# A fused retention and Mish feed-forward kernel on one core: four buffers for scaled v, w_in's third piece in two, one first-layer block in another PSUM bank, six products no longer in halves

## The chip, the core and the metric

The kernel runs on one core of a Trainium2 chip. A core has a matrix engine (TensorE, "PE" in the profile; its weight loads have a row of their own, "PEld"), three engines for elementwise work (VectorE "DVE", ScalarE "ACT", GpSimd "POOL") and a queue engine (SyncE, "SP") that mostly issues transfers. TensorE writes to PSUM, eight banks of 128 partitions x 512 float32; the other operands live in SBUF. The engines run beside each other and wait for each other by semaphores; transfers between the device's memory and SBUF run on 16 DMA engines that all queues share. The metric is the device time of one execution in microseconds (us), the median of several.

## The reference, cut to what matters

```python
# q, k, v: (8, 8, 576, 64) float32: batch, head, position, head dimension
scores = np.matmul(q, k.transpose(0, 1, 3, 2)) / np.sqrt(64)
gamma  = 1.0 - 2.0 ** (-5.0 - np.arange(8))
Dmat   = np.where(rel >= 0, gamma[:, None, None] ** rel, 0.0)   # rel = i - j
attn   = np.matmul(scores * Dmat, v)
x = attn.transpose(0, 2, 1, 3).reshape(4608, 512)
h = x @ w_in                               # (512, 2048)
g = h * np.tanh(np.log1p(np.exp(h)))       # Mish
out = g @ w_out                            # (2048, 512)
```

There is no softmax: a score is only multiplied by a power of gamma that falls with the distance. So a row can be computed from its own block of positions and a running sum ("state") of k times v over the earlier ones, with gamma's power split into a factor for q and its inverse for v. That v, times its inverse factor, is "scaled v", `vs` in the kernel.

## The kernel before, in words

**Tiling.** The 4608 token rows are 36 chunks of 128 rows, nine tiles of four chunks. The first eight chunks (tiles 0 and 1) are the first 128 positions of each of the eight batches, and have code of their own (`f_...`); the other 28 go through `step_p` (scale q and cast q and k to `qks`, on DVE), `step_v` (scale v to `vs`, line 301: on DVE for chunks below 20, on POOL from 20 on), `step_t` (transposes, on TensorE for chunks below 18, by transfers from SP after that), and, two chunks at a time, `visit`. A visit makes on TensorE the new states of chunks n+2 and n+3 (`states`, line 392), the outputs of chunks n and n+1 from scores and scaled v (`outputs`, line 451), their rest from the states (`outputs_end`, line 468) and the next scores (`step_s`, line 337): several hundred small matmuls within some 1.4 us. The outputs go to two PSUM banks and are cast from there to `xT`, one half on ACT and one on DVE (`outputs_copy`, line 480).

**The feed-forward layers.** `g1(t, f)` makes one 128 x 512 block of the first layer for tile t: four accumulating products over the 512 input features into a PSUM bank `hp`, then Mish on ACT (line 541) into `gT`. There are 16 blocks to a tile. `g2` makes the second layer for 128 rows from 16 products. After the visit, `g1` needs the two `hp` banks that the visit's outputs held.

**Products in halves.** `product` issues one matmul with 512 columns, or, while a counter `halved[0]` is above zero and the product is neither the first nor the last of its sum, two matmuls with 256 columns each, each with a weight load of its own (lines 520 to 523). Work and result are the same; the program has one load and one matmul more.

**The PSUM pools** are `ps_sc` (tiles of two banks, two of them), `ps_st` (one bank), `ps_h` (two banks, `hp`) and `ps_o` (one bank, `ops`).

**The order of the work** is written out by hand: the calls stand in the order in which each engine gets them, and a tile pool makes an instruction wait where it would overwrite a buffer that is still read. The POOL queue holds the casting transfers (w_in, w_out and the first q and k, float32 in memory and bf16 in SBUF), all the other loads of q, k and v, some elementwise work and, from chunk 20 on, `step_v`. Its transfers share eight semaphores in turn, so that each waits until the one eight places before it has landed. w_in arrives in pieces along its 2048 columns: 256, 256, 512 (the third), 512 and 512; block f of `g1` needs columns 128f to 128f + 127.

**Where the change is.** Pool `tok` (line 66) holds `vs`, five buffers. At the start (lines 665 to 669) the 16 blocks of tile 0 run:

```python
    for f in range(2):
        g1(0, f, 2, begun[f])
    for f in range(2, nF):
        halved[0] = 2 if f > 3 else 1
        g1(0, f)
```

In the loop over the tiles from 2 on, `n` is the chunk whose visit is next and `w` the place within its eight steps. At `w` of 0 and 1 `step_v` is called for chunks n+2 and n+3, a little after the visit of n-2; the visit of n comes at `w` of 6; at `w` of 5 DVE scales one v for a state (`f_state`, line 254, result `v0s`), for n from 16 to 22 only.

Of the kernel before, what the change touches and what calls it, by code (L numbers as in the profile page):

```python
# [9 lines left out]
F32 = mybir.dt.float32  # L10
# [6 lines left out]
def kernel(  # L17
# [21 lines left out]
    P = 128  # L39
# [5 lines left out]
    NCH = 4  # L45
# [17 lines left out]
    wpool = ctx.enter_context(tc.tile_pool(name="weights", bufs=1))  # L63
    first = ctx.enter_context(tc.tile_pool(name="first", bufs=1))
    io = ctx.enter_context(tc.tile_pool(name="io", bufs=PF))
    tok = ctx.enter_context(tc.tile_pool(name="tok", bufs=5))
    tr = ctx.enter_context(tc.tile_pool(name="tr", bufs=4))
    xp = ctx.enter_context(tc.tile_pool(name="xp", bufs=2))
    gp = ctx.enter_context(tc.tile_pool(name="gp", bufs=2))
# [4 lines left out]
    ps_h = ctx.enter_context(tc.tile_pool(name="ps_h", bufs=2, space=PS))  # L74
    ps_o = ctx.enter_context(tc.tile_pool(name="ps_o", bufs=1, space=PS))
# [9 lines left out]
    def load_w_in(f0, n):  # L85
        nc.gpsimd.dma_start(out=w_in_t[:, :, ds(f0, n)], in_=w_in_r[:, :, ds(f0, n)])
# [22 lines left out]
    def load_first_v(b):  # L109

        if b < 4:
            pair = stage[:, ds(8 + 2 * b, 4), :].bitcast(F32).rearrange("p a (c d) -> p (a c) d", d=D)
        else:
            pair = first.tile([P, 2 * H, D], F32, name="vpair", bufs=2)
        for e in range(2):
            v0[b + e] = pair[:, ds(H * e, H), :]
        nc.gpsimd.dma_start(out=pair, in_=v[ds(b, 2), :, 0:P, :].rearrange("b h p d -> p (b h) d"))
# [23 lines left out]
            load_first_qk(0, i, b)  # L141
    load_first_v(0)
    load_first_v(2)
    for f0, n in ((0, 256), (256, 256), (512, 512)):
        load_w_in(f0, n)
    mask = consts.tile([P, 64], F32)
    lg = [math.log(1.0 - 2.0 ** (-5.0 - h)) for h in range(H)]
# [108 lines left out]
    def load_k0(b):  # L256
        k0r[b] = first.tile([P, H, D], F32, name="k0r", bufs=2)
        nc.gpsimd.dma_start(out=k0r[b], in_=k[b, :, 0:P, :].rearrange("h p d -> p h d"))

    def cast_k0(b, copy=nc.scalar.copy):  # L260
        k0[b] = first.tile([P, H, D], BF16, name="k0", bufs=3)
        copy(k0[b], k0r[b])
# [3 lines left out]
    def load(n, gate=None):  # L266
        if n >= n_chunks:
            return
        b, c = chunks[n]
        qkr = io.tile([P, 2, H, D], F32, name="qkraw")  # L270
        vr = io.tile([P, H, D], F32, name="vraw", bufs=7)
        live[n] = {"qkr": qkr, "v": vr}
        for t, src in ((qkr[:, 0], q), (qkr[:, 1], k), (vr, v)):
            if c < 4:
                ins = nc.gpsimd.dma_start(  # L275
                    out=t, in_=src[b, :, ds(P * c, P), :].rearrange("h p d -> p h d"))
                if gate is not None:
                    behind(ins, gate)
                    gate = None
            else:  # L280
                for e in range(2):
                    nc.gpsimd.dma_start(
                        out=t[ds(64 * e, 64)],
                        in_=src[b + e, :, ds(512, 64), :].rearrange("h p d -> p h d"))
# [151 lines left out]
    def run(jobs, *how):  # L436
        while jobs:
            jobs.pop()(*how)
# [45 lines left out]
    def hold(n):  # L484

        nc.gpsimd.tensor_copy(held[:, n % 2:n % 2 + 1], live[n]["qk"][:, 1, NP - 1, P - 1:P])  # L486

    def visit(n, banks, copies, between=None):


        units, early = states(n + 2)
        if units:
            units[0]()
        both = outputs(n, banks)
        seen = written(outputs_end(n, both, 0))
        if units:
            step_s(n + 2)
        elif between:
            between()
        for unit in units[1:early]:  # L500
            unit()
        outputs_end(n, both, 1, seen)
        for unit in units[max(early, 1):]:
            unit()
        outputs_copy(n, both, copies)
        if units:
            step_m(n + 2)

    outs = {}
    halved = [0]  # L510
# [4 lines left out]
    def product(to, w, x, first, last):  # L515
        if first or last or not halved[0]:
            newest[0] = nc.tensor.matmul(to, lhsT=w, rhs=x, start=first, stop=last)  # L517
            return
        halved[0] -= 1
        n = x.shape[-1] // 2  # L520
        for j in range(2):
            nc.tensor.matmul(to[:, ts(j, n)], lhsT=w, rhs=x[:, ts(j, n)], start=False, stop=False,  # L522
                             skip_group_check=True)

    def g1_half(f):
        hp = ps_h.tile([P, NCH * P], F32, name="hp")
        n = NCH * P // 2
        for c in range(KC):
            nc.tensor.matmul(hp[:, 0:n], lhsT=w_in_t[:, c, ts(f, P)], rhs=xts[0][:, c, 0:n],
                             start=(c == 0), stop=(c == KC - 1))  # L530
        return hp

    def g1(t, f, parts=1, begun=None):
        if t not in gts:
            gts[t] = gp.tile([P, nF, NCH * P], BF16, name="gT")
        hp = ps_h.tile([P, NCH * P], F32, name="hp") if begun is None else begun
        n = NCH * P // parts
        for j in range(0 if begun is None else 1, parts):
            for c in range(KC):
                product(hp[:, ts(j, n)], w_in_t[:, c, ts(f, P)], xts[t][:, c, ts(j, n)], c == 0, c == KC - 1)  # L540
        done = nc.scalar.activation(gts[t][:, f, :], hp, AX.Mish)  # L541
        if (t, f) in gated:
            load(gated[t, f], done)
            queued[0] += 1
# [18 lines left out]
    def stores(copy=nc.vector.tensor_copy):  # L563
        while ready:
            store(*ready.pop(), copy)
# [35 lines left out]
    def att(n, steps):  # L601
        if n >= n_chunks:
            return
        for step in steps:
            {"P": step_p, "V": step_v, "T": step_t}[step](n)
# [33 lines left out]
    begun = [g1_half(0), g1_half(1)]  # L639
# [25 lines left out]
    for f in range(2):  # L665
        g1(0, f, 2, begun[f])
    for f in range(2, nF):
        halved[0] = 2 if f > 3 else 1
        g1(0, f)
    for i in range(2):  # L670
        f_mix(0, i)
# [1 line left out]
    for i in range(nF):  # L673
        for step in steps.get(i, "").split():
            n = int(step[1])
# [77 lines left out]
    for t in range(2, nT + 1):  # L753
        for i in range(nF):
            n, w = NCH * (t + 1) + i // 8 * 2, i % 8
            if w == 2 and n in cast_at:
                cast_k0(cast_at[n])
            if w == 2:
                run(casts, act)
                halved[0] = {20: 32}.get(n, 0)  # L760
            if w == 6 and n + 4 == NPE:
                load_k0(3)
                att(n + 4, "T")
                att(n + 5, "T")
            if w == 6 and n < n_chunks:
                visit(n, ((ps_h, "hp"), (ps_h, "hp")), (act, dve), lambda: g2(t - 1, i))
            if w == 0:
                stores(act if n == N0 + 4 else dve)
                run(sums)
            if w == 7 and n + 2 == NPE:  # L770
                stores()
            if w in (0, 1) and n + 2 < NPE:
                att(n + 2 + w, "P")
            if w in (4, 5) and n + 4 >= NPE:
                stores()
                att(n + w, "P")
            if w in ((3, 4) if n + 2 < NPE else (0, 1)):
                att(n + 2 + (w in (1, 4)), "V")
            if w == 5 and 16 <= n < 24:
                f_state(1, n // 2 - 8, nc.vector)  # L780


            if w == 7 and n + 4 == NPE:
                hold(n + 4)
                hold(n + 5)
                more_loads(n + 7)
            if w == 1 and NPE < n + 2 < n_chunks:
                hold(n + 2)
            if w == 1 and n + 2 >= NPE:
                more_loads(n + 7)  # L790
                if t in (3, 4):
                    load_k0(2 * t - 2 + i // 8)
            if w in (4, 5) and n + 2 < NPE:
                att(n - 2 + w, "T")
            stores()


            if t == 2:
                if w == 6:
                    g2(1, 8 + i // 2)  # L800
                g1(t, i)
                if i % 2 and w != 7:
                    g2(1, 8 + i // 2)
            elif t == nT:
                if i < 12:
                    g2(t - 1, i)
            elif w == 6:

                last = n < n_chunks <= n + 2
                g2(t - 1, i + last)  # L810
                g1(t, i)
                if NPE < n + 4 < n_chunks:
                    for x in (4, 5):
                        step_t(n + x, newest[0])
            elif w == 7 and n < n_chunks <= n + 2:
                g1(t, i)
            elif i % 4 == 0:
                g1(t, i)
                g1(t, i + 1)
                g2(t - 1, i)  # L820
            else:
                if i % 4 != 1:
                    g1(t, i)
                g2(t - 1, i)
# [32 lines left out]
```

## Time and profile before

| | |
|---|---|
| median of three runs | 300.78 us (300.23 to 300.98) |
| the profiled execution | 302.5 us, of which its span (first to last instruction) 300.8 |
| TensorE busy | 288.6 us, 96% of the span |
| VectorE, ScalarE, GpSimd busy | 147.6, 134.9, 133.3 us |
| granted TensorE clock | 1.000 over the span |
| moved by DMA | 47.45 MB, 160 GB/s over the span |
| instruction queue (q8) | 27 transfers, 0.44 MB |

A line of a time view has the start and the duration in us, engine, line of the kernel, operation, output <- inputs, shape and the number of instructions merged into it; in brackets stands how long the engine was idle before it and what ended that. "issue" means that nothing in the profile explains the wait. A matmul's end is modelled, so neighbouring matmuls overlap in the view; the distance between their starts (0.216 us for 512 columns in a dense stretch, since four follow in 0.86 us) is the better measure.

### The profile page before, as it was taken

How to read it: one execution, taken by the hardware profiler on the slowest of the kernel's cores; microseconds unless marked ns; L12 is line 12 of the kernel's file. 1: busy time of each engine (PE TensorE's matmuls, PEld its weight loads, DVE VectorE, ACT ScalarE, POOL GpSimd, SP SyncE). 2: the span in 40 equal slices, each digit the busy share in tenths (PEclk: the TensorE clock that was granted, in tenths of full speed). 3: DMA queues.
4: the chain of work that ended last, by engine and by line, in shares of the span. 5: the costliest groups of instructions: out<-in, count | busy, mean ns of one | idle time of the engine just before them, and what ended most of it. 6: DMA issues, size and time to landing. Idle time of an engine off the chain costs nothing.

```text
span 300.8 us, 7911 instructions
## 1 busy us (share of the span) xinstructions
PE 288.6 (96%) x3450; PEld 157.1 (52%) x3488; DVE 147.6 (49%) x237; ACT 134.9 (45%) x221; POOL 133.3 (44%) x173
## 2 busy tenths in 40 slices
PE   7889999999899999999999999999999999999995
PEld 3456787555455545456744454545454544444443
DVE  5722547597939548472849363727363312011011
ACT  5557325876557552534353435343535342433200
POOL 8675856767464294836575724656110000000000
PEclk9999999999999999999999999999999999999999
DMA  7999999999998679878977858876714110110131
GB/s 152 210 206 206 203 238 222 340 227 198 250 218 218 141 205 206 212 188 151 213 192 199 202 129 144 210 179 173 107 37 105 37 37 35 37 35 35 51 91 71
DMA packets 39619, 47.45 MB, mean 158 GB/s; under 512 B 21792, under 2 KB 28448, under 8 KB 39584
## 3 DMA queue, kind: packets, MB, share of 16 engines
q0 software_dynamic: 14896, 32.25, 48.7%
q1 hardware_dynamic: 24544, 14.49, 20.5%
q8 instruction: 27, 0.44, 0.7%
q10 hardware_dynamic: 144, 0.20, 0.2%
q14 instruction: 8, 0.07, 0.1%
HBM read 38.80 MB, written 9.44 MB: 160 GB/s over the span
## 4 chain that ended last, share of the span: by engine, by line
PE 84%; DVE 5%; DMA 4%; issue 3%; POOL 3%; DVEq 0%; POOLq 0%
PE hp L517 38%; PE ops L517 29%; PE hp L522 5%; DMA w_in_t<-in_moe_w_in_dram 4%; DVE qks L294 3%; PE ops L522 2%; PE sc L315 1%; PE hp L585 1%; PE sc L337 1%; POOL gT L106 1%; PE st L522 1%; PE sc L392 1%; PE hp L468 1%; DVE v0s L254 1%; PE hp L451 1%
## 5 line engine op out<-in xcount | busy, mean ns | idle before, releaser
L517 PE MATMUL hp<-xT,w_in_t 128*128 128x512 bf16 (+1 forms) x512 | 128.2, 376 | 3.1 <-DVE xT L480 1.0
L541 ACT ACTIVATE gT<-hp 128x512 bf16<-128x512 f32 x144 | 86.0, 598 | 94.2 <-PE hp L517 87.7
L517 PE MATMUL ops<-w_out_t,gT 128*128 128x512 bf16 x417 | 103.2, 379 | 1.9 <-issue 1.9
L517 PEld LDWEIGHTS <-w_in_t 128*128 128x128 bf16 x532 | 51.7, 98 | 57.0 <-issue 2.3
L517 PEld LDWEIGHTS <-gT 128*128 128x128 bf16 x484 | 46.1, 98 | 52.7
L593 DVE COPY res<-ops 128x512 f32<-128x512 f32 x28 | 19.3, 690 | 88.4 <-PE ops L517 88.4
L294 DVE TENSOR_TENSOR qks<-qkraw,gqk 128x512 bf16<-128x512 f32 x56 | 42.6, 815 | 4.1 <-DMA qkraw<-in_k_dram 4.1
L275 POOL DMA_DIRECT2D qkraw<-in_q_dram x24 | 21.5, 894 | 13.4 <-ACT gT L541 8.4
L486 POOL COPY held<-qkT 128x1 bf16<-128x1 bf16 x10 | 1.9, 187 | 51.6 <-DMA qkT<-qks 51.6
L301 POOL TENSOR_TENSOR vs<-vraw,gv 128x512 bf16<-128x512 f32 x16 | 18.3, 1148 | 10.7 <-PE hp L451 10.5
L275 POOL DMA_DIRECT2D vraw<-in_v_dram x24 | 21.2, 884 | 3.1 <-DMA vpair<-in_v_dram 1.5
L275 POOL DMA_DIRECT2D qkraw<-in_k_dram x24 | 21.2, 884 | 2.5 <-DMA w_out_t<-in_moe_w_out_dram 1.3
L480 ACT CAST xT<-hp 128x512 bf16<-128x512 f32 x14 | 8.2, 586 | 28.1 <-PE hp L468 26.9
L480 DVE CAST xT<-hp 128x512 bf16<-128x512 f32 x13 | 8.9, 688 | 21.9 <-PE hp L468 16.7
L428 DVE TENSOR_TENSOR total<-sc,total 128x256 f32<-128x256 f32 x40 | 16.9, 422 | 1.0
L343 DVE TENSOR_TENSOR sm<-sc,mask 128x1024 bf16<-128x1024 f32 x14 | 17.0, 1214 | 0.6 <-PE sc L337 0.6
L522 PEld LDWEIGHTS <-gT 128*128 128x128 bf16 x152 | 14.5, 98 | 3.0
L522 PE MATMUL hp<-xT,w_in_t 128*128 128x256 bf16 x96 | 14.6, 272 | 0.0
L522 PEld LDWEIGHTS <-w_in_t 128*128 128x128 bf16 x96 | 9.4, 98 | 6.1 <-issue 0.6
L431 ACT CAST ssb<-total 128x768 bf16<-128x768 f32 (+3 forms) x13 | 11.7, 897 | 1.7 <-DVE total L428 1.6
L517 PE MATMUL hp<-w_out_t,gT 128*128 128x512 bf16 x49 | 12.0, 379 | 0.2 <-issue 0.2
L392 PE MATMUL sc<-vs,qks 64*64 64x64 bf16 x384 | 9.7, 197 | 0.0
(120 smaller groups left out, 259.1 us busy)
## 6 DMA issues: line engine op xcount, KB each, us to landing
out_dram<-res SPq DMA_DIRECT2D x31, 256.0 KB, 3.8
qkraw<-in_q_dram POOLq DMA_DIRECT2D x24, 256.0 KB, 5.0
qkraw<-in_k_dram POOLq DMA_DIRECT2D x24, 256.0 KB, 5.4
vraw<-in_v_dram POOLq DMA_DIRECT2D x24, 256.0 KB, 5.7
w_out_t<-in_moe_w_out_dram POOLq DMA_DIRECT2D x4, 512.0 KB, 11.2
k0r<-in_k_dram POOLq DMA_DIRECT2D x8, 256.0 KB, 7.1
w_in_t<-in_moe_w_in_dram POOLq DMA_DIRECT2D x3, 512.0 KB, 11.1
gT<-in_k_dram POOLq DMA_DIRECT2D x8, 128.0 KB, 6.8
```

Source lines behind the costliest of these rows:

```text
L275: ins = nc.gpsimd.dma_start(out=t, in_=src[b, :, ds(P * c, P), :].rearrange("h p d -> p h d"))
L294: nc.vector.tensor_tensor(slots[:, :, y], heads[:, :, y], factors[:, :, y].unsqueeze(3).to_broadcast([P, NP, 2, D]), op=OP.mult)
L301: engine.tensor_tensor(vs, live[n]["v"], gv[:, c, :].unsqueeze(2).to_broadcast([P, H, D]), op=OP.mult)
L343: nc.vector.tensor_tensor(sm.rearrange("p e x n i -> p (e x n) i"), live[n]["sc"].rearrange("p e x n i -> p (e x n) i"), mask.unsqueeze(1) ...
L392: ins = nc.tensor.matmul(to, lhsT=ks, rhs=vs, start=(x is not None or j == 0 and p == 0), stop=True, skip_group_check=True)
L428: nc.vector.tensor_tensor(new[:, k], st[:, j, x], total[b], op=OP.add)
L431: casts.append(lambda copy: copy(lows[:, 0:k], new[:, 0:k]))
L480: copy(xts[t][:, :, ds(P * s, 2 * P)].rearrange("p h (x j i) -> p j h x i", x=2, j=2)[:, j], both[j])
L517: newest[0] = nc.tensor.matmul(to, lhsT=w, rhs=x, start=first, stop=last)
L522: nc.tensor.matmul(to[:, ts(j, n)], lhsT=w, rhs=x[:, ts(j, n)], start=False, stop=False, skip_group_check=True)
L541: done = nc.scalar.activation(gts[t][:, f, :], hp, AX.Mish)
L593: copy(ot, ops)
```

## The change

Four edits. Scaled v gets four buffers instead of five. The third piece of w_in (columns 512 to 1023) is loaded by two transfers of 256 columns. Block 2 of tile 0's first layer is accumulated in the `ops` bank instead of an `hp` bank. And six products that were issued as two halves are issued whole: one each in blocks 4, 5 and 6 of tile 0, and three of the 32 that follow in the stretch after `n == 20`.

```diff
-    tok = ctx.enter_context(tc.tile_pool(name="tok", bufs=5))
+    tok = ctx.enter_context(tc.tile_pool(name="tok", bufs=4))
...
-    for f0, n in ((0, 256), (256, 256), (512, 512)):
+    for f0, n in ((0, 256), (256, 256), (512, 256), (768, 256)):
         load_w_in(f0, n)
...
-        hp = ps_h.tile([P, NCH * P], F32, name="hp") if begun is None else begun
+        if begun is not None:
+            hp = begun
+        elif (t, f) == (0, 2):
+            hp = ps_o.tile([P, NCH * P], F32, name="ops")
+        else:
+            hp = ps_h.tile([P, NCH * P], F32, name="hp")
...
     for f in range(2, nF):
-        halved[0] = 2 if f > 3 else 1
+        halved[0] = 2 if f > 6 else 1
         g1(0, f)
...
             if w == 2:
                 run(casts, act)
-                halved[0] = {20: 32}.get(n, 0)
+                halved[0] = {20: 29}.get(n, 0)
```

## The prediction

> **What bounds the kernel now.** I read the engines' totals first, then TensorE's waits, then the time view around each, then the chain of waits. TensorE is busy for 96% of the span at full clock:
>
> ```profile
> PE 288.6 (96%) x3450; PEld 157.1 (52%) x3488; DVE 147.6 (49%) x237; ACT 134.9 (45%) x221; POOL 133.3 (44%) x173
> ```
>
> So only the places where TensorE stands still can be won. Its waits after the start (engine, line, what it waited for; us, times, longest):
>
> ```profile
> PE hp L517 <- DVE xT L480: 1.0, 3, 0.4
> PE hp L517 <- issue: 0.8, 2, 0.6
> PE hp L517 <- DMA w_in_t<-in_moe_w_in_dram: 0.4, 1, 0.4
> ```
>
> From about 21 us the chain of waits runs through TensorE to the end, save three stretches through DVE that end in these three xT waits. What TensorE gains early therefore reaches the end, unless one of those stretches starts from something else. It does not: each begins with a DVE copy released by a product (110.38 us, behind "PE ops"). I size a standstill by the distance between the starts of neighbouring matmuls or weight loads, less the normal 0.216 us (0.11 behind a half).
>
> *Place 1, the third piece of w_in.* Block 4 needs it; POOL's row shows when the next piece has landed, since its transfer waits for that:
>
> ```profile
> 19.71 0.59 PE L517 MATMUL hp<-xT,w_in_t 128*128 128x512 bf16 x2
> 20.68 0.39 PE L517 MATMUL hp<-xT,w_in_t 128*128 128x512 bf16 x1 [0.38 <-DMA w_in_t<-in_moe_w_in_dram]
> 23.71 0.59 POOL L106 DMA_DIRECT2D gT<-in_k_dram  x1 [0.90 <-PE hp L517]
> ```
>
> The two products start at 19.71 and 19.92, so block 4 could start at 20.14 and starts at 20.68: 0.54 lost.
>
> *Place 2, the instruction stream.* Block 2 of tile 2 stops in the middle of one sum, with nothing to wait for; a smaller stop lies inside the visit at 68 us:
>
> ```profile
> q8 instruction: 27, 0.44, 0.7%
> 68.10 0.26 PEld L337 LDWEIGHTS <-qkT 64*64 64x64 bf16 x21 [0.20 <-issue]
> 79.85 0.59 PE L517 MATMUL hp<-xT,w_in_t 128*128 128x512 bf16 x2
> 81.04 1.46 PE L517 MATMUL hp<-xT,w_in_t 128*128 128x512 bf16 x6 [0.59 <-issue]
> ```
>
> 27 transfers for TensorE's 6,976 loads and matmuls are one per 258 instructions, so a block has about 256. Counted in the trace, the loads that come late at 68.10 and 81.04 are the 736th and the 992nd: 256 loads, so 512 instructions, two blocks apart. I read both as the first instructions of blocks that came too late. The transfer before the second ran from 78.31 to 79.62, after two dense visits (67.2 and 74.3 us) had used some 500 instructions. The distance between the loads is 0.97, so 0.75 is lost there and about 0.3 at 68.10.
>
> *Place 3, POOL's scaling against DVE's scaling.* The visit at 114 us:
>
> ```profile
> 113.85 2.22 POOL L301 TENSOR_TENSOR vs<-vraw,gv 128x512 bf16<-128x512 f32 x2
> 113.87 0.43 PE L451 MATMUL hp<-sm,vs 64*64 64x64 bf16 x32
> 114.09 2.53 DVE L254 TENSOR_TENSOR v0s<-vpair,gv 128x512 bf16<-128x512 f32 x1
> 116.54 0.68 DVE L480 CAST xT<-hp 128x512 bf16<-128x512 f32 x1
> 117.27 1.02 PE L517 MATMUL hp<-xT,w_in_t 128*128 128x512 bf16 x4 [0.27 <-DVE xT L480]
> ```
>
> The scaling v0s takes 0.68 elsewhere and 2.53 here, ending just behind POOL's two scalings: it stood until POOL was done. The cast behind it frees the hp bank late. The same happens at 147.93 and 163.82. The starts are 0.64, 0.56 (behind a half) and 0.79 apart: 0.42 + 0.45 + 0.57 = 1.44 lost. At 130 us the order is the other way and nothing is lost:
>
> ```profile
> 130.00 0.68 DVE L254 TENSOR_TENSOR v0s<-vpair,gv 128x512 bf16<-128x512 f32 x1
> 130.00 1.58 POOL L301 TENSOR_TENSOR vs<-vraw,gv 128x512 bf16<-128x512 f32 x1 [1.08 <-PE hp L451]
> 130.69 0.69 DVE L480 CAST xT<-hp 128x512 bf16<-128x512 f32 x1
> ```
>
> DVE was first, POOL took 1.58 in place of 1.06, and the cast from PSUM ran at its usual 0.69 beside POOL.
>
> **The change part by part.**
>
> *w_in's third piece in two.* Columns 512 to 767 land without waiting for the rest. From the landing of the second piece (18.34, block 2's load) to that of the third (20.64) lie 2.3 us; half is 1.15 to 1.35, so the first half lands at about 19.6, before 20.14, and the second near 20.8, before block 6 (20.14 + 1.73 = 21.87). The runs become shorter, and that costs:
>
> ```profile
> 13.00:16.00 3.00, 2.92 (x43) 1.45 (x43) 2.81 (x6) 1.65 (x4) 3.00 (x6) 1.00 1.36 193
> 16.00:20.50 4.50, 4.00 (x37) 2.58 (x32) 0.85 (x2) 2.43 (x5) 2.81 (x4) 1.00 1.26 207
> ```
>
> The last column is GB/s. From 13 to 16 us mostly the 256-column pieces move, later the wider ones: 193 against 207, 7% of some 2.3 us, 0.13 to 0.17. The fourth piece then lands at 23.66 + 0.15 and block 8, which before started at 20.68 + 4 x 0.868 = 24.15, starts at about 23.84 in place of the 23.6 that TensorE could reach. Gain 0.31. Bounds: 0.54 with no cost of the short runs; a loss of 1.5 if a piece of 256 columns always takes the 2.1 us between the first two landings (16.24 at the latest, and 18.34). I take 0.31, since the rate over 3 us is the nearer row: the first two pieces also queue behind v. On POOL one more issue (0.8) falls into its idle 2.38 before 12.77. Behind it the eight semaphores turn by one place: the last q load of the first group now waits for the second piece (18.4 in place of 16.5) and w_out's first for the new halves (about 19.6 and 20.8 in place of 18.58 and 20.92, with POOL's v0s behind each). I cost that at nothing: until 26.3, when w_in's last piece lands, the DMA engines work through a full queue, so these only join it later. Were that cover gone, the q transfer would be 1.9 late at DVE's copy of 28.36, whose result TensorE wants at 30.9; 0.5 of that is spare.
>
> *Block 2 in the ops bank.* Its first matmul started at 18.41, its weights were there at 18.34; ops has been free since 16.8. Gain 0 to 0.07; I take 0. The next user of ops is g2 at 33.97.
>
> *Six products whole.* Eight halves take 0.87 where four whole take 0.86, 0.003 for each pair: 6 x 0.003 = 0.02. What counts is the place of the blocks: three loads and three matmuls fewer stand ahead of 68 and 81 us. Each block then begins six instructions later in the work. [...] Bounds: 0.75, and a loss of 0.3 (the smaller stop once more, if another block comes late); I take 0.65, worked from the stop itself. The other three, near 140 us, move later blocks; by the trace every transfer of that queue after 83 us ends 3 us or more ahead of its block's first instruction: nothing.
>
> [...]
>
> *Four buffers for vs.* On DVE (chunks below 20) the buffer's last reader is an earlier visit, which ended 5 us or more ahead: no wait. On POOL, scaling n+2 overwrote the v of n-3, now that of n-2, so it waits for the outputs of the visit of n-2, as that of n+3 did before. The row of 130.00 shows a scaling start 0.40 behind the first such output (129.60). At the three visits that gives 114.27, 145.10 and 160.67. DVE's v0s starts at 114.09, at 144.75, and, without the lock on the qks ahead of it (4 x 0.78 behind 157.38, as at 111), at 160.4: first each time, by 0.18, 0.35 and 0.25. Then it takes 0.68, the cast follows as soon as the outputs are complete (115.1 in place of 116.54), over 1 us ahead of need. Gain 1.44. Behind the later scalings on POOL stand the copy that waits for transposes (121.22, 5.15 idle before it) and then loads: the 1 us of delay is covered by that idle time. Bounds: 1.44, and a loss of 0.9: POOL first at all three, two scalings of 1.05 from 114.27, v0s 0.55 and the cast 0.69 behind them to 117.6, against 116.85 when TensorE wants the bank: 0.8 each, 2.4 in place of 1.44.
>
> **Sum.** 0.31 + 0.02 + 0.65 + 1.44 = 2.4 off the span of 300.8: 298.4, or 300.1 with the 1.7 that lie around it in the profiled 302.5. The unprofiled median, 300.78, is the length of the span; I take off it 2.3, as the stop at 81 hangs on one transfer's queueing.
>
> **The rivals.**
> - *Partly.* One group fails: POOL is first after all (margins 0.18 to 0.35), or the stop at 81 us only moves. 300.78 - 0.96 (no gain of vs) to - 1.65 (none of the stream): 299.1 to 299.8, and 300.3 where both fail in part. For it: narrow margins, times from one execution.
> - *Nothing.* The unprofiled executions, 1.7 shorter than the profiled one, lack these stops, if the recording itself brings them about: only the 0.3 of the start, 300.5. Against it: the xT stops follow from the order on POOL and DVE, not from traffic.
> - *Slower.* The scalings of v now fall on the cast of each of the eight visits from 16 to 30. If POOL's lock stops the cast too, it ends at 0.40 + 2.1 + 0.69 = 3.2 behind the first output, where TensorE wants the bank at 2.98: 0.25 at five visits, and 0.8 at the three with a v0s, 3.65 in place of 1.44. With the other gains of 1.0 that is 302.0. It decides from the point where the cast waits 0.3 us for POOL. Against it: the cast of 130.69 took 0.69 beside POOL.
>
> **How the numbers follow.** Forecast 0.53 (297.7 to 299.4), partly 0.25 (299.1 to 300.3), nothing 0.12 (300.2 to 301.1), slower 0.10. About 0.3%, 0.9 us, is what a measurement can tell: faster is below 299.88, which takes the forecast and half of the second, 0.66; slower above 301.68, 0.10. The range runs from 297.7 to 300.9: it leaves out the slower case and some of nothing's.
>
> **What would show it.** Block 4 starts near 20.1 and block 8 near 23.8; the stop in tile 2 shrinks from 0.75 to 0.1 or so, three products later; POOL's scalings come in pairs behind the outputs of visits, v0s takes 0.68 at all four, and no xT wait of TensorE is left. It is wrong if v0s still takes 2.5, if a new "issue" stop stands elsewhere between 60 and 90 us, or if block 8 waits beyond 24.2.

## The result and the profile after

The changed kernel takes 299.61 us in the median (299.07 to 301.55) against 300.88 us for the kernel before (299.67 to 303.74): a ratio of 0.9956, with a 95% interval from 0.9938 to 0.9974. It is faster by 1.3 us, where 2.3 were forecast. The two recorded executions differ by more, 302.5 us (span 300.8) against 299.74 us (span 298.0), that is by 2.8 in both measures.

The engines' totals after:

```profile
PE 290.9 (98%) x3482; PEld 156.1 (52%) x3482; DVE 136.0 (46%) x237; ACT 134.8 (45%) x221; POOL 132.8 (45%) x174
```

DVE is busy for 11.6 us less than in the record of before, with as many instructions. Of that, 7.4 lie in the scalings of q and k (line 294) and 3.7 in v0s (line 254): they wait less inside their own time (the longest takes 0.69 and 0.68, in place of 2.52 and 2.53).

*Place 1.* The time view around blocks 3 to 5 of tile 0, and GpSimd's next k issue:

```profile
19.36 0.81 PE L517 MATMUL hp<-xT,w_in_t 128*128 128x512 bf16 x3
20.01 0.38 PE L522 MATMUL hp<-xT,w_in_t 128*128 128x256 bf16 x2
20.23 0.81 PE L517 MATMUL hp<-xT,w_in_t 128*128 128x512 bf16 x3
23.71 0.59 POOL L106 DMA_DIRECT2D gT<-in_k_dram  x1 [0.45 <-PE hp L517]
```

The third product of the first line, at 19.79, is the first of block 4: it follows without a wait, 0.9 us earlier than before (20.68). The traces also hold the updates of the transfers' semaphores, and they give the landings. Here the second piece landed at 18.00, the halves of the third at 19.30 and 20.63, the fourth at 23.17; in before the second landed at 18.30, the third at 20.64, the fourth at 23.18. So in these two records the split made neither the third piece as a whole nor the fourth later. The k issue at 23.71, the same in both, comes 0.53 behind the landing that it waits for. Block 8 starts at 23.26 (block 4 plus four times 0.868) in place of 24.15. But the lead shrinks again at 30.6, where the chain of waits (start, us, what) and TensorE's time view show a new bound:

```profile
18.56 9.80 DMA gT<-in_q_dram
28.45 2.08 DVE qbx L175
```

```profile
30.58 0.62 PE L190 MATMUL sc<-ident,qbx 128*128 128x128 bf16 x8 [0.21 <-DVE qbx L175]
```

The chain of before ran through w_in to 20.64 and from there through TensorE alone. Now it runs through a q transfer and a DVE copy, and TensorE waits for that copy: its first matmul starts 0.59 behind the product ahead of it (29.99) in place of 0.22, so 0.37 is lost. At 34 us the changed kernel is 0.52 ahead.

*Place 2.* The time view of block 2 of tile 2, where TensorE had stood for 0.75:

```profile
78.22 1.03 PE L517 MATMUL ops<-w_out_t,gT 128*128 128x512 bf16 x4
79.09 1.89 PE L517 MATMUL hp<-xT,w_in_t 128*128 128x512 bf16 x8
80.81 1.03 PE L517 MATMUL ops<-w_out_t,gT 128*128 128x512 bf16 x4
```

Eight products run through. The stop at 68 us is gone too.

*Place 3.* GpSimd's scalings, DVE's scaling v0s and its cast at the visit of 113 us, and then at that of 128 us:

```profile
111.82 0.68 DVE L254 TENSOR_TENSOR v0s<-vpair,gv 128x512 bf16<-128x512 f32 x1
112.91 2.05 POOL L301 TENSOR_TENSOR vs<-vraw,gv 128x512 bf16<-128x512 f32 x2
113.53 0.69 DVE L480 CAST xT<-hp 128x512 bf16<-128x512 f32 x1 [1.02 <-PE hp L468]
...
128.02 2.04 POOL L301 TENSOR_TENSOR vs<-vraw,gv 128x512 bf16<-128x512 f32 x2 [0.86 <-PE hp L451]
128.70 0.69 DVE L480 CAST xT<-hp 128x512 bf16<-128x512 f32 x1 [0.89 <-PE hp L468]
```

v0s takes 0.68 and begins 0.89 to 1.09 ahead of GpSimd (at all four places). GpSimd's scalings come in pairs, from 128 us on behind the outputs of the visit (line 451), and the cast runs at 0.69 in the middle of them. It waits for the outputs' last products (line 468) alone. No wait of TensorE for xT is left.

How late the record of before is against that of after, measured at the same weight load in both, gives the whole difference: 0.52 at 34 us, 0.76 at 69, 1.52 at 80, 1.99 at 117, 2.23 at 148, 2.81 at 164, and 2.78 at the end. So in these two executions the start was worth 0.52, the instruction stream 0.24 + 0.76, and the three xT stops 0.43 + 0.24 + 0.58.

### The profile page after: what moved, and what is told of

The parts are those of the page before. It is cut to its first block, busy times and chain, and to the rows that moved or that the text cites. A ratio compares the mean times of both kernels' runs of the same rounds, so it can differ in the third digit from the quotient of the medians.

```text
span 298.0 us, 7938 instructions
## 1 busy us (share of the span) xinstructions
PE 290.9 (98%) x3482; PEld 156.1 (52%) x3482; DVE 136.0 (46%) x237; ACT 134.8 (45%) x221; POOL 132.8 (45%) x174
## 4 chain that ended last, share of the span: by engine, by line
PE 89%; DMA 6%; POOL 2%; DVE 1%; issue 1%; POOLq 0%; DVEq 0%
PE hp L517 39%; PE ops L517 32%; PE hp L522 4%; DMA gT<-in_q_dram 3%; DMA w_in_t<-in_moe_w_in_dram 3%; PE ops L522 2%; PE sc L337 1%; PE sc L392 1%; PE hp L468 1%; PE sc L315 1%; PE hp L451 1%; PE hp L590 1%; POOL gT L106 1%; PE st L522 1%; POOL gT L117 1%; PE st L392 1%
## 5 line engine op out<-in xcount | busy, mean ns | idle before, releaser
L517 PE MATMUL hp<-xT,w_in_t 128*128 128x512 bf16 (+1 forms) x533 | 129.7, 376 | 0.0
L517 PE MATMUL ops<-w_out_t,gT 128*128 128x512 bf16 x432 | 106.8, 379 | 0.0
L294 DVE TENSOR_TENSOR qks<-qkraw,gqk 128x512 bf16<-128x512 f32 x56 | 35.2, 683 | 4.5 <-DMA qkraw<-in_k_dram 4.5
L301 POOL TENSOR_TENSOR vs<-vraw,gv 128x512 bf16<-128x512 f32 x16 | 16.3, 1041 | 21.3 <-PE hp L451 21.3
L522 PE MATMUL hp<-xT,w_in_t 128*128 128x256 bf16 x86 | 13.3, 273 | 0.0
L517 PE MATMUL hp<-w_out_t,gT 128*128 128x512 bf16 x52 | 12.7, 379 | 0.0
```

What stands on the lines that cost most here:

```text
L294: nc.vector.tensor_tensor(slots[:, :, y], heads[:, :, y], factors[:, :, y].unsqueeze(3).to_broadcast([P, NP, 2, D]), op=OP.mult)
L301: engine.tensor_tensor(vs, live[n]["v"], gv[:, c, :].unsqueeze(2).to_broadcast([P, H, D]), op=OP.mult)
```

## The experiments

Each kernel was compared with the kernel before on the chip on which it ran itself. The median of before on those chips was 300.43, 300.90 and 300.93, so kernels of different groups are compared by their ratios. The first group is the first four below, the second the next four, the third the last four; of these groups only the second holds the changed kernel itself. A ratio is not exactly the quotient of the two medians (0.9970 below, where 299.80 / 300.90 is 0.9963), so differences under 0.3 us can't be read from ratios. "The record" is the one execution of a kernel whose trace was kept.

### Four buffers alone

```diff
-    tok = ctx.enter_context(tc.tile_pool(name="tok", bufs=5))
+    tok = ctx.enter_context(tc.tile_pool(name="tok", bufs=4))
```

> The kernel before with four buffers for scaled v instead of five, and nothing else. Theory A (each stop is as long in every execution as in the one recorded): the three waits of TensorE for xT near 117, 148 and 164 us go, v0s takes 0.68 at all four places, and the time falls by 1.4 us, ratio 0.995. Theory B (the recorded execution of before, 302.5, was a long one of its kind, and the stops behind POOL's scalings are shorter or missing in others): the profile shows the same order of the scalings, but the median falls by 0.3 to 0.9 us only, ratio 0.997 to 0.999. Theory C (the gain of the whole change lies at the start and in the instruction stream alone): no change within 0.2%.

Median 300.01, ratio 0.9981 (0.9968 to 0.9995): theory B. The visit of this kernel at 144 us, in the time view:

```profile
143.32 0.68 DVE L254 TENSOR_TENSOR v0s<-vpair,gv 128x512 bf16<-128x512 f32 x1
144.24 2.04 POOL L301 TENSOR_TENSOR vs<-vraw,gv 128x512 bf16<-128x512 f32 x2 [1.04 <-PE hp L451]
145.05 0.69 DVE L480 CAST xT<-hp 128x512 bf16<-128x512 f32 x1 [1.05 <-PE hp L468]
```

v0s is over 0.24 before GpSimd begins, and the cast takes 0.69 beside GpSimd's scalings, clear of the lock (DVE standing until GpSimd's scalings are done, as v0s did for 2.53 in place of 0.68 at 114 us in before). No xT wait is left.

### The split of w_in alone

```diff
-    for f0, n in ((0, 256), (256, 256), (512, 512)):
+    for f0, n in ((0, 256), (256, 256), (512, 256), (768, 256)):
```

> The kernel before with the third piece of w_in loaded in two, and nothing else. Theory A: block 4 starts at about 20.1 without a wait, block 8 at 23.8, and 0.3 us is won: ratio 0.999. Theory B (the copy qbx, which waits for the q transfer at 28.4, takes most of it back): block 8 starts 0.3 to 0.6 earlier, but TensorE waits for qbx near 30.6 for most of it, and the second layer starts 0.1 to 0.5 us earlier: ratio 0.998 to 1.000. The stop in tile 2 stays (0.5 us or more), and the waits for xT stay.

Median 300.52, ratio 1.000 (0.9974 to 1.0026): too wide to tell 0.3 us. In the record block 4 runs on without a wait, as expected, but TensorE does not wait for qbx. I had expected the stop at the 992nd load to stay, and it is not there; one of 0.45 stands at the 736th. Of the three xT stops one is left, 0.34. It shows the lock with five buffers, at the visit just quoted:

```profile
141.55 0.88 POOL L258 DMA_DIRECT2D k0r<-in_k_dram  x1
142.45 2.29 POOL L301 TENSOR_TENSOR vs<-vraw,gv 128x512 bf16<-128x512 f32 x2
142.76 2.53 DVE L254 TENSOR_TENSOR v0s<-vpair,gv 128x512 bf16<-128x512 f32 x1
145.21 0.68 DVE L480 CAST xT<-hp 128x512 bf16<-128x512 f32 x1
```

Here, with five buffers, GpSimd scales as soon as its load issues are out (142.43), without a wait for a product of the visit. It was 0.31 ahead of v0s. At 112 us of the same execution it was 0.15 behind (112.34 against 112.19), v0s took 0.68, and nothing was lost.

### The six products whole, alone

```diff
-        halved[0] = 2 if f > 3 else 1
+        halved[0] = 2 if f > 6 else 1
...
-                halved[0] = {20: 32}.get(n, 0)
+                halved[0] = {20: 29}.get(n, 0)
```

> The kernel before with the six products whole, and nothing else. Theory A (the block of instructions that came too late is needed three products later, its request leaves at the same time): the stop of 0.75 in block 2 of tile 2 shrinks to about 0.1 and stands three products later, the smaller one at 68 us stays near 0.3, and the time falls by 0.65 us, ratio 0.998. Theory B (the delay of the instruction transfer changes from execution to execution by more than these three products): a stop between 0 and 0.8 is seen at the shifted place, and the median changes by less than 0.3 us. The waits for xT stay.

Median 300.63, ratio 1.0007 (0.9990 to 1.0025): theory B. The record has no stop at the 992nd load and one of 0.42 at the 736th.

### Two products more in halves

```diff
-        halved[0] = 2 if f > 3 else 1
+        halved[0] = 2 if f > 1 else 1
```

> The kernel before with two products more in halves (one in each of blocks 2 and 3 of tile 0), so that every later block of instructions begins two products earlier in the work: the other direction. Theory A: the stop in tile 2 stands two products earlier and grows by 2 x 0.216 = 0.43 to some 1.2 us; the time rises by 0.4 us, ratio 1.0015. Theory B (the delay of the transfer changes by more than that between executions): a stop between 0 and 1.2, median within 0.3 us of before's. The waits for xT stay.

Median 300.64, ratio 1.0001 (0.9980 to 1.0023). The record agrees with theory A on the place and is larger than its size:

```profile
78.88 1.03 PE L517 MATMUL ops<-w_out_t,gT 128*128 128x512 bf16 x4
81.13 1.24 PE L517 MATMUL hp<-xT,w_in_t 128*128 128x512 bf16 x5 [1.23 <-ACT ssb L431]
```

The stop stands ahead of the block's first product, two products earlier than before's, at the 992nd load again; 1.60 lies between the loads, so 1.38 is lost. (The line names ACT's copy ssb. That it was the instruction stream is argued, from the count of loads and from the transfer on its queue that ended at 79.75: the load came 1.38 behind it, and the 992nd load of before 1.42 behind its own.) There is no stop at 736, and one of 0.33 at the 864th load. The median is theory B's.

### The changed kernel once more

> The changed kernel once more, beside the kernels that leave one part of it out, on the same chip. Theory A (the forecast: 2.3 us): ratio 0.992. Theory B (the first comparison: 1.3 us, because the recorded execution of before was a long one): ratio 0.994 to 0.997. Its profile shows whether the stop in the instruction stream is gone for good (A: nothing over 0.15 at the 992nd load, 0.3 at the 736th) or varies (B: anything from 0 to 0.8 at either), and whether the waits for xT are gone again (both theories: yes).

Median 299.80, ratio 0.9970 (0.9956 to 0.9984): theory B, a gain of 1.1 us. The record has stops of 0.34 at the 736th load and of 0.33 at the 864th, none at the 992nd, and no xT wait.

### The changed kernel with five buffers

```diff
-    tok = ctx.enter_context(tc.tile_pool(name="tok", bufs=4))
+    tok = ctx.enter_context(tc.tile_pool(name="tok", bufs=5))
```

> The changed kernel with five buffers for scaled v, as before. Theory A (three xT stops of the recorded length in each execution): 1.4 us above the changed kernel. Theory B (four buffers alone were worth 0.4 to 0.7 us): 0.4 to 0.7 above the changed kernel, ratio to before 0.996 to 0.998. Theory C (the parts help only together): no gain left, ratio 1.000. In the profile v0s takes 2.5 again at three places in A, at one to three in B.

Median 300.07, ratio 0.9976 (0.9958 to 0.9993), 0.27 above the changed kernel on the same chip: below theory B's lower end, far from A. The intervals of the two ratios overlap. One xT stop is back, 0.57 near 161 us. There v0s took 0.68 itself but began at 159.98, since the scalings of q and k ahead of it on DVE had stood behind GpSimd (three in 4.58 from 155.48, where four took 3.02 from 109.15).

### Split and bank, without the rest

```diff
-    for f0, n in ((0, 256), (256, 256), (512, 512)):
+    for f0, n in ((0, 256), (256, 256), (512, 256), (768, 256)):
...
-        hp = ps_h.tile([P, NCH * P], F32, name="hp") if begun is None else begun
+        if begun is not None:
+            hp = begun
+        elif (t, f) == (0, 2):
+            hp = ps_o.tile([P, NCH * P], F32, name="ops")
+        else:
+            hp = ps_h.tile([P, NCH * P], F32, name="hp")
```

> The kernel before with the third piece of w_in in two and block 2 in the outputs' bank. Theory A (the bank is worth 0 to 0.07): the same as the split alone, ratio 0.999 to 1.000. Theory B (with the earlier piece, blocks 2 to 4 wait for a bank whose Mish is late, 0.2 us in the run of the split alone, and the bank takes that wait away): 0.2 to 0.5 us below the split alone, ratio 0.998. In the profile of B no product of blocks 2 to 4 waits for gT.

Median 300.20, ratio 0.9981 (0.9967 to 0.9995). That is B's number, but the interval of the split alone reaches over it, so the pair does not decide. The record has two xT stops (0.49 and 0.13) and none in the instruction stream.

### The changed kernel with the halves of before

```diff
-        halved[0] = 2 if f > 6 else 1
+        halved[0] = 2 if f > 3 else 1
...
-                halved[0] = {20: 29}.get(n, 0)
+                halved[0] = {20: 32}.get(n, 0)
```

> The changed kernel with the six products in halves, as before. Theory A (the place of the instruction blocks decides the stop): the stop at the 992nd load is back with 0.5 to 0.8 us, ratio to before 0.65 us nearer to 1 than the changed kernel's. Theory B (the stop varies from execution to execution, and three products do not decide it): within 0.3 us of the changed kernel, and the stops at the 736th and 992nd load lie anywhere between 0 and 0.8.

Median 299.80, ratio 0.9959 (0.9943 to 0.9975), the same median as the changed kernel's on this chip: theory B. The record has no stop of either kind. From split and bank (300.20, on the same chip too) this kernel differs by the four buffers alone, and it is 0.40 below it.

### The changed kernel without the bank

```diff
-        if begun is not None:
-            hp = begun
-        elif (t, f) == (0, 2):
-            hp = ps_o.tile([P, NCH * P], F32, name="ops")
-        else:
-            hp = ps_h.tile([P, NCH * P], F32, name="hp")
+        hp = ps_h.tile([P, NCH * P], F32, name="hp") if begun is None else begun
```

> The changed kernel with block 2 back in a bank of hp. Theory A (the bank is worth 0 to 0.07 us): the same as the changed kernel, ratio to before 0.996 to 0.997. Theory B (the split is worth something only with the bank, since the split alone came out at 1.000 and split and bank together at 0.998): 0.4 to 0.7 above the changed kernel, ratio 0.998 to 0.999. In the profile, B shows a wait of blocks 2 to 4 for gT of 0.2 us or more that is not made good by 31 us.

Median 299.63, ratio 0.9957 (0.9943 to 0.9972): theory A by time. The record shows the wait that the bank takes away:

```profile
18.24 0.38 PE L517 MATMUL hp<-xT,w_in_t 128*128 128x512 bf16 x1 [0.25 <-ACT gT L541]
```

In this execution TensorE came to the transposes at 30.38 without a wait for qbx, which had been ready at 29.8, so no later wait made the 0.25 good in this record. The median does not show it.

### The changed kernel without the split

```diff
-    for f0, n in ((0, 256), (256, 256), (512, 256), (768, 256)):
+    for f0, n in ((0, 256), (256, 256), (512, 512)):
```

> The changed kernel with the third piece of w_in in one transfer of 512 columns. Theory A (0.31, as forecast): 0.3 us above the changed kernel, ratio to before 0.997 to 0.998. Theory B (the recorded executions: those with the split reach 34 us between 0.6 ahead of the changed kernel's record and level with it, those without it 0.2 to 0.8 behind): 0.6 to 0.9 us above the changed kernel, ratio 0.998 to 0.999, and block 4 waits 0.3 to 0.6 for w_in again.

Median 299.78, ratio 0.9961 (0.9943 to 0.9979): 0.15 above the kernel without the bank on the same chip, so smaller than both theories. The load of block 4 waits 0.25 for its piece, and between the products 0.05 is lost, less than in before, since block 2 began at 18.87 only, behind a late vb at the start.

### GpSimd's first scalings earlier

```diff
     for i, b in ((1, 2), (1, 3), (0, 2), (0, 3)):
         load_first_qk(1, i, b)
-    for b in (2, 3):
-        f_state(0, b)
+        if (i, b) == (1, 2):
+            for s in (2, 3):
+                f_state(0, s)
```

> The changed kernel with GpSimd's scalings of the second pair of first states (2.05 us) between the two k loads ahead of them, in 2 us that GpSimd spends idle, in place of behind the q loads, where they run beside DVE's copy qbx and stretch it from 0.4 to 2.0. Theory A (TensorE's wait for qbx near 30.3, 0.4 to 0.5 in three of the recorded executions and none in others, goes): qbx takes 0.4 to 0.6, no weight load near 30 us comes late, and 0.2 to 0.5 us is won on the changed kernel. Theory B (another transfer or qkT takes its place): qbx is short, TensorE waits elsewhere before 35 us, median within 0.2.

```profile
24.21 2.05 POOL L254 TENSOR_TENSOR v0s<-gT,gv 128x512 bf16<-128x512 f32 x2
```

```profile
28.34 0.66 DVE L175 COPY qbx<-gT 128x1024 bf16<-128x1024 bf16 x1 [11.87 <-DMA gT<-in_q_dram]
```

```profile
30.52 0.61 PE L190 MATMUL sc<-ident,qbx 128*128 128x128 bf16 x8
```

The copy takes 0.66 in place of 2.07, so GpSimd's scalings were what stretched it. TensorE does not wait for it, but it also came late here (30.52): a copy of 2.07 would have ended at 30.41. That the wait of the changed kernel's record goes is worked out: a copy of 0.66 from 28.45 ends at 29.11, ahead of the 30.21 at which TensorE wanted it there. The median, 299.65 (ratio 0.9961, 0.9945 to 0.9976), is level with the two kernels above: theory B's time. In this record TensorE waits at two places where that of after does not: 0.64 for the second piece of w_in ahead of block 2 (18.37), and 0.45 inside the visit at 99 us, where the profile names a queue instruction of SP. Whether the edit brings these about is not shown. So no version here is shown to beat the changed kernel.

### The kernel before once more

> The kernel before itself, once more, as a run among the others: what the comparison makes of no change, and a second recorded execution. Theory A (the stops are those of the first record): 0.75 and 0.3 late at the 992nd and 736th load, and three waits for xT of 0.4 to 0.6. Theory B (they differ between executions, and the first record was a long one): other sizes, in sum 0.5 to 1.5 in place of 2.5, and a span nearer to the median less 1.7, some 299. The ratio is 1.000 within its interval in both.

Median 300.75, ratio 0.9993 (0.9977 to 1.0010). The record, span 299.2, has block 4's wait at the start, nothing in the stream and one xT stop:

```profile
20.66 0.39 PE L517 MATMUL hp<-xT,w_in_t 128*128 128x512 bf16 x1 [0.60 <-DMA w_in_t<-in_moe_w_in_dram]
...
79.61 1.89 PE L517 MATMUL hp<-xT,w_in_t 128*128 128x512 bf16 x8
...
162.21 1.02 PE L517 MATMUL hp<-xT,w_in_t 128*128 128x512 bf16 x4 [0.41 <-DVE xT L480]
```

Its sum of stops behind 34 us is 0.6, against 2.25 in the first record: theory B.

### What the records have in common

Lateness at 34 us against the record of after, then what was lost in the instruction stream and at the xT stops (us, at the same weight loads). Two stops fall under none of these heads: 0.51 near 47 us in "after once more", behind a late cast of v, and 0.45 near 99 us in "scalings earlier". "Parts" are those of the change that the kernel has: V four buffers, S split, O bank, W whole products.

| kernel | parts | start | stream | xT | ratio |
|---|---|---|---|---|---|
| before | | 0.52 | 1.00 | 1.25 | |
| before once more | | 0.50 | 0 | 0.61 | 0.9993 |
| two more in halves | | 0.31 | 1.71 | 0.95 | 1.0001 |
| whole alone | W | 0.81 | 0.42 | 0.93 | 1.0007 |
| split alone | S | -0.62 | 0.45 | 0.34 | 1.0000 |
| split and bank | S O | -0.50 | 0 | 0.62 | 0.9981 |
| five buffers | S O W | -0.35 | 0 | 0.57 | 0.9976 |
| four buffers alone | V | 0.23 | 0.72 | 0 | 0.9981 |
| without the split | V O W | 0.48 | 0 | 0 | 0.9961 |
| without the bank | V S W | -0.21 | 0 | 0 | 0.9957 |
| halves of before | V S O | -0.49 | 0 | 0 | 0.9959 |
| after once more | all | -0.60 | 0.67 | 0 | 0.9970 |
| after | all | 0 | 0 | 0 | 0.9956 |
| scalings earlier | all | -0.07 | 0 | 0 | 0.9961 |

With five buffers the xT stops sum to 0.34 to 1.25, 0.75 in the mean of seven; with four they are zero in all seven. In all seven v0s begins 0.89 to 1.16 ahead of GpSimd at each of the four visits; with five, GpSimd is first at some and DVE at others, often by a few tenths. The stops in the stream come and go in kernels of both kinds. The column of the start is not a measure of the split: "whole alone" and "without the split" were already 1.1 late at the first load of w_in (16 us), behind a late vb, and the second piece, which the split leaves alone, landed anywhere between 17.36 and 18.32 us.

A least-squares fit of all the times of these kernels (the last row left out, two more in halves too) by the four parts, with a level for each chip, gives for four buffers -0.70 us (standard error 0.13), the split -0.21 (0.14), the bank -0.34 (0.19), the whole products -0.06 (0.13). It takes the parts as adding up, so it is a rough division of the 1.3.

## Why the prediction was right or wrong

The direction was right, at 299.61 within the range. That says little, since the range reached up to 300.9, past the median of before. The time lies 1.1 above the forecast, outside the forecast case's own 297.7 to 299.4 and inside that of "partly" (299.1 to 300.3), and only half for the reasons given there: the whole products' 0.65 is not seen, but GpSimd was not first, and the gain of the four buffers was there, smaller in the median than in the record that I priced it from.

**The step that failed is under "Sum"**: the profiled execution of 302.5 was taken for an ordinary one, with 1.7 around its span that the unprofiled median would lack. Each execution's time is its span plus about 1.7 (299.74 against 298.0 here, 300.87 against 299.2 for before once more). So the first record was 1.6 longer than the median of before, and that surplus was made of the very stops that I summed: 2.25 of them stand behind 34 us in that record, 0.6 in the second record of the same kernel, which is 1.6 shorter. Taking 2.3 off the median charged the median for stops that it has in part only.

**Four buffers for vs**: the mechanism is right in each point (order, 0.68, pairs behind the outputs, no xT wait), and the lead of v0s, worked out as 0.18 to 0.35, is 0.89 or more. The term of 1.44 is mis-sized: 1.25 even in that record, since the stop at 148 us was 0.24 and not 0.45 (I had subtracted a half's distance), 0.75 in the mean of the records, 0.70 in the fit, and 0.4, 0.4 and 0.3 by the medians of the three pairs that differ by it alone on one chip. I had asked who comes first in one execution; with five buffers that is a race of a few tenths, which falls both ways (GpSimd 0.31 ahead at 142 us and 0.15 behind at 112 us in the record of the split alone).

**The place of the instruction blocks**: the count was right. Stops stand at the 736th, 864th or 992nd load whatever the number of halves ahead (with two more halves, two products earlier in the work). From the 864th load to the 992nd the traces have 5.8 us with the halves of before and 6.4 with the whole products: 0.62 more, where three distances of 0.216 make 0.65. But no run shows the term of 0.65: with the halves of before only one record of six has a stop at that load. No trace shows when a block is asked for, only when its transfer runs. The transfer for that load started 3.84 behind the 864th load in the first record of before (78.32 against 74.48) and 2.38 behind it in that of after (76.13 against 73.75); over the records it started between 74.9 and 78.4 us, so its start varies by more than the edit adds. No record has more than two stops in the stream; the nine in all are of 0.24 to 1.38.

**w_in's third piece**: block 4 runs on, and the gain to block 8 was 0.9 in the record, not 0.31. I had read the fourth piece's landing from the k issue, as 23.66; by its semaphore it landed at 23.18, and at 23.17 with the split, so the 0.15 for short runs was not paid and nothing held block 8. What I left out is what is late next: I compared qbx with before's 30.9 and not with TensorE's own earlier arrival at 30.2, and 0.37 went back there. The size is open. At 34 us the records with the split are level with after or up to 0.62 ahead, those without it 0.23 to 0.81 behind, but part of that is older than the third piece, as said above. The fit says 0.21, and the split alone gave nothing measurable. I can't reconcile these. The turn of the semaphores cost nothing, as taken: the q transfer landed at 28.4 in both.

**Block 2 in ops**: I took 0 within 0 to 0.07. The record of before already had a wait for gT at 18.41, and up to 0.25 of such a wait is seen without the bank; leaving it out cost nothing measurable, the fit says 0.34 (0.19). Not settled.

**The rivals**: "slower" fell as argued: the casts took 0.69 beside GpSimd's 2.04. "Nothing" was half right: the medians hold part of the stops (four buffers win 0.3 to 0.7), but not the sum that one record had. Nor does the recording itself bring the stops about each time: 5 of the 14 recorded executions are shorter than their kernel's median, and 8 have no stop in the stream.

## What to carry to other kernels

A stop that hangs on a race (two engines a few tenths apart, a transfer that queues behind others) is to be priced by how often it happens, not by its length in one trace; when the profiled execution is longer than the median by as much as its stops, they are the first suspects. Tie a low-priority instruction to an event of the critical engine, as the buffer count does here for GpSimd's scalings, and the race is decided the same way each time (in all seven records with four buffers v0s came first, by 0.89 to 1.16). And when an early stage gets faster, compare the next stage's inputs with the new arrival time.

## What was unexpected of the hardware

The copy qbx, bf16 to bf16 within SBUF, took 1.96 to 2.09 beside GpSimd's scalings and 0.66 without them: not only operations with two inputs, such as v0s, were held up. v0s from 142.76 in the record of the split alone, 0.31 behind GpSimd, took 2.53 and ended 0.55 behind GpSimd's second scaling; the cast from PSUM beside GpSimd's scalings took 0.69 (128.70 in the record of after).

In the nine stops of the stream a block's first load came 1.38 to 1.64 us after the last packet of the transfer that I read as its own: 1.42 and 1.38 at the 992nd load, 1.54 and 1.56 at the 864th, 1.45 to 1.64 at the 736th. Where the transfer ended 1.6 or more ahead of need no record shows a stop.
